# Retention and a gelu feed-forward on one core: spreading the retention steps over the first blocks, with steps 10-13 turned by DMA, the state cast on ScalarE and the last row block in halves

## The chip, the cores and the metric

The kernel runs on one core of a Trainium2 chip. TensorE (PE in the profile) multiplies, VectorE (DVE) and ScalarE (ACT) do the elementwise work, GpSimd (POOL) and SyncE (SP) issue transfers. Each engine takes its own list of instructions in order, and semaphores tie the lists together. The metric is the time of the whole kernel on the device, in microseconds (us); lower is better.

## The reference

```python
# q, k, v: (8 batches, 8 heads, 576 positions, 64)
scores = (q @ k.transpose(0, 1, 3, 2)) / sqrt(64)
gamma  = 1 - 2.0 ** (-5 - arange(8))                    # one decay per head
D      = where(i - j >= 0, gamma[h] ** (i - j), 0)      # causal decay
attn   = (scores * D) @ v
x = attn.transpose(0, 2, 1, 3).reshape(4608, 512)
h = x @ w_in                                            # (4608, 2048)
out = (h / (1 + exp(-1.702 * h))) @ w_out               # (4608, 512)
```

## The kernel before

**Retention in steps.** Each batch's 576 positions are five pieces of 128, 128, 128, 128 and 64 rows, so there are 40 *steps*; step n is piece n % 5 of batch n // 5. The decay is split into a factor per query row (`gq`), a factor per key row (`vfac`, multiplied into v by `scale_v`, line 314) and a causal mask. A running *state* (keys times values, summed over pieces in `zacc`) carries the earlier pieces. For a step the kernel needs:

- q and k *turned*, so that the 64 head values lie on partitions. Before step 14 (`PE_TURNS`) that is eight transposes on TensorE into the bank `psW` and an evacuation on ScalarE (`transposes`, line 338, and `evac_t`, line 344; together `turn`). From step 14 on SP issues two DMA transposes (`dma_turn`, line 545). The result is in one of four `qk` buffers.
- the scores on TensorE (line 375) and the mask on VectorE (line 397): together `intra`.
- `values_quarters` (lines 416 to 435): mask times v, the state's update and the earlier state's contribution, into `psV`, in two parts with the next step's `intra` between them.
- `finish`: `evac_o` (line 535) writes the step's rows into `xT` times `gq`; `evac_z` (lines 506 to 521) adds the new state to `zacc` and, after the first three pieces, casts `zacc` to the bf16 buffer `zq` that the next step reads. After a batch's last step `finish` also has POOL load a later batch.

`burst(n)` puts these together: step n-1's values, step n's scores and mask, the turn of step n+1 (or the DMA turn of step n+3), `finish(n-1)` and `scale_v(n+1)`.

**Feed-forward in blocks.** The 4608 rows are nine *blocks* of 512. A block's first product (`hidden`, line 593, 16 units of four matmuls of 512 columns) goes through the gelu on ScalarE (line 598) into `gT`. `hidden_half` (line 611) does the same in 16 units of eight matmuls of 256 columns, the first eight for the block's first half of rows. The second product (`project`, line 627, 16 units: four row blocks r, four quarters g) ends each row block with a copy out of PSUM on VectorE (line 635) and an output transfer on SP.

**Banks.** Hidden units take turns over `psH0`, `psH1` and, with three in rotation, `psU`, by a counter `hcount` that runs through the whole kernel. `project(0)` uses `psU`, `psH0`, `psH1` and `psU` again for its fourth row block; in later blocks row blocks alternate between `psU` and `psW`. The last block uses four banks.

**Order.** The order is written out by hand: each call records instructions on every engine's list, and `Rec` works out the semaphore waits from what is read, written and which bank is touched. Steps 0 to 3 come first, then block 0's first product, block 0's second product with steps 4 to 7, block 1's first product with bursts 8 to 13, and then regions:

```python
between = {0: 8, 2: 9, 5: 10, 8: 11, 11: 12, 14: 13}
for i in range(NF):
    hidden_half(1, i // 8, 2 * (i % 8))
    if i in between:
        burst(between[i])
```

`region(c)` (line 751) interleaves block c-1's second product with block c's first in 32 units, in the repeating pattern O H O H O O H H (O for `project`, H for `hidden`), and places its four or five bursts evenly. Region 2 holds bursts 14 to 18; regions run to 8, and the last block's second product ends the kernel.

Of the kernel before, what the change touches and what calls it, by code (L numbers as in the profile page):

```python
# [6 lines left out]
AF = mybir.ActivationFunctionType  # L7
# [15 lines left out]
NCH = (B * S) // 512  # L23
NF = FF // 128
NST = 3
NQK = 4
PE_TURNS = 14
QK_SCALE = 1.0 / math.sqrt(DH)


# [99 lines left out]
def bass_retnet_parallel__then__act_gelu_quick_kernel(  # L130
# [9 lines left out]
    R = Rec()  # L140
    es = ExitStack()
    with es:
        def sb(name, shape, dtype):
            return es.enter_context(nc.sbuf_tensor(name, shape, dtype))

        def ps(name, shape, dtype=FP32):
            return es.enter_context(nc.psum_tensor(name, shape, dtype))
# [12 lines left out]
        zacc = sb("zacc", [P, HP, DH], FP32)  # L160
        zq = [sb(f"zq{i}", [P, HP, DH], BF16) for i in range(2)]
# [9 lines left out]
        w_out_sb = sb("w_out_sb", [P, NF, DM], BF16)  # L171
        gT = [sb(f"gT{i}", [P, NF, 512], BF16) for i in range(2)]
        osb = [sb(f"osb{i}", [P, 512], FP32) for i in range(3)]

        psW = ps("psW", [P, 512])
        psT = psW.ap().bitcast(BF16).rearrange("p (a h n) -> p a h n", a=2, h=HP)
        psS = ps("psS", [P, 2, HP, 128])
        psV = ps("psV", [P, 2, 512])
# [135 lines left out]
        def scale_v(n, eng="DVE"):  # L314
            b, c = divmod(n, NC)
            sl = b % NST
            t = st_v[:, sl, c, :].rearrange("p (h d) -> p h d", d=DH)
            f = vfac[min(b, 1)][:, :, c : c + 1].to_broadcast([P, H, DH])
            R.op(eng, lambda e: e.tensor_tensor(t, t, f, ALU.mult),  # L319
                 r=[("vfac", min(b, 1))], w=[("v", sl, c)])  # L320
# [26 lines left out]
        def turn_first_keys():  # L347

            transposes(4, [(1, st_k, "k", 1, 0)])
            R.op("ACT", lambda e: e.activation(qk[4 % NQK][:, 1], psT[:, 1], AF.Copy),  # L350
                 w=[("qk", 4 % NQK, 1)], ps=["W"])
# [154 lines left out]
        def evac_z(n):  # L506
            c = n % NC
            if n >= NC:
                new = psV[:, :, 256:384]
                acc = zacc.ap().rearrange("p (u t) d -> p u (t d)", u=2)  # L510
                z = zq[c % 2].ap().rearrange("p (u t) d -> p u (t d)", u=2)
                if c == 0:
                    R.op("DVE", lambda e: e.tensor_copy(acc, new), w=["zacc"], ps=["O", "Z"])
                elif c < 3:
                    R.op("DVE", lambda e: e.tensor_tensor(acc, acc, new, ALU.add),
                         w=["zacc"], ps=["O", "Z"])
                if c < 3:
                    R.op("DVE", lambda e: e.tensor_copy(z, acc), r=["zacc"], w=[("zq", c % 2)])
                else:
                    R.op("DVE", lambda e: e.tensor_tensor(z, acc, new, ALU.add),  # L520
                         r=["zacc"], w=[("zq", c % 2)], ps=["O", "Z"])
                return
            for hh in range(2):
                rows = slice(64 * hh, 64 * hh + 64)
                R.op("ACT", lambda e, rows=rows: e.activation(
                    zs[c % 2][rows, :, rows], psZ[rows, :, 0:64], AF.Copy),
                    w=[("zs", c % 2, hh)], ps=["Z"])
# [17 lines left out]
        def dma_turn(n):  # L545
            for a, t, nm, sl, c in sides(n):
                rows = P if nm == "k" else ROWS[c]
                R.op("SP", lambda e, a=a, t=t, rows=rows, sl=sl, c=c: e.dma_start_transpose(
                    out=qk[n % NQK][:, a, :, 0:rows], in_=t[0:rows, sl, c, :]),
                    r=[(nm, sl, c)], w=[("qk", n % NQK, a)], dma=("turn", n % NQK, a))  # L550

        def turn(n):
            transposes(n)
            evac_t(n)
# [5 lines left out]
        def finish(n):  # L560
            evac_o(n)
            if n % NC < 4:
                evac_z(n)
            b = n // NC + NST
            if n % NC == 4 and b < B:
                load_entry(b)

        def burst(n):
            if n > NC:
                values_quarters(n - 1)  # L570
            else:
                intra(n)
                values(n - 1)
            if n + 1 < PE_TURNS:
                turn(n + 1)
            if PE_TURNS <= n + 3 < NSTEP:
                dma_turn(n + 3)
            finish(n - 1)
            if n + 1 < NSTEP:
                scale_v(n + 1)  # L580


        hcount = [0]
# [2 lines left out]
        def hidden(c, f, rotate=2):  # L586
            bank, key = hbanks[hcount[0] % rotate]
            hcount[0] += 1
            toks = {(t0 // S, (t0 % S) // 128) for t0 in range(512 * c, 512 * c + 512, 64)}

            def fn(e):
                for a in range(4):
                    i = e.matmul(bank.ap(), w_in_sb[:, a, 128 * f : 128 * f + 128],  # L593
                                 xT[:, a, 512 * c : 512 * c + 512],
                                 start=(a == 0), stop=(a == 3))
                return i
            R.op("PE", fn, r=[("w_in", f // 4)] + [("xT", *x) for x in sorted(toks)], ps=[key])
            R.op("ACT", lambda e: e.activation(gT[c % 2][:, f, :], bank.ap(),  # L598
                                               AF.Gelu_apprx_sigmoid),
                 w=[("gT", c % 2, f)], ps=[key])  # L600
# [20 lines left out]

        ocount = [0]

        def project(c, r, g, bank, key):
            def fn(e):
                for f in range(4 * g, 4 * g + 4):
                    i = e.matmul(bank, gT[c % 2][:, f, 128 * r : 128 * r + 128], w_out_sb[:, f, :],  # L627
                                 start=(f == 0), stop=(f == NF - 1))
                return i
            R.op("PE", fn, r=[("w_out", g)] + [("gT", c % 2, f) for f in range(4 * g, 4 * g + 4)],  # L630
                 ps=[key])
            if g == 3:
                m = ocount[0] % 3
                ocount[0] += 1
                R.op("DVE", lambda e: e.tensor_copy(osb[m].ap(), bank), w=[("osb", m)], ps=[key])  # L635
                row0 = 512 * c + 128 * r
                R.op("SP", lambda e: e.dma_start(out[row0 : row0 + 128, :], osb[m].ap()),
                     r=[("osb", m)], dma=("osb", m))


        constants_first()
# [66 lines left out]
        for b in (1, 2):  # L708
            load_entry(b)

        wide = [(psU.ap(), "U"), (psH[0].ap(), ("H", 0)), (psH[1].ap(), ("H", 1)),
                (psV[:, 0, :], "O")]
# [8 lines left out]
        def burst_4():  # L721
            intra(4)
            turn_first_keys()
            turn(5)
            scale_v(5)

        def burst_7():
            values_quarters(6)
            finish(6)
            turn(8)  # L730
            scale_v(8)

        regroup()
        between = {6: turn_4, 8: burst_4, 10: lambda: burst(5), 12: lambda: burst(6),
                   14: burst_7}
        units = [(r, g) for g in range(4) for r in range(3)] + [(3, g) for g in range(4)]
        for i, (r, g) in enumerate(units):
            project(0, r, g, *wide[r % 3])
            if i in between:
                between[i]()  # L740
        between = {0: 8, 2: 9, 5: 10, 8: 11, 11: 12, 14: 13}
        for i in range(NF):
            hidden_half(1, i // 8, 2 * (i % 8))
            if i in between:
                burst(between[i])

        def last_step(c):
            t = 512 * (c + 1) - 1
# [2 lines left out]
        def region(c):  # L751
            units = []
            for r in range(4):
                o = [("O", c - 1, r, g) for g in range(4)]
                h = [("H", c, f) for f in range(4 * r, 4 * r + 4)]
                units += [o[0], h[0], o[1], h[1], o[2], o[3], h[2], h[3]]
            if c + 1 < NCH:
                bursts = list(range(last_step(c) + 2, last_step(c + 1) + 2))
            else:
                bursts = []  # L760
            at = {}
            for i, n in enumerate(bursts):
                at[int((i + 0.5) * (len(units) - 2) / len(bursts))] = n
            for i, u in enumerate(units):
                if u[0] == "H":
                    hidden(u[1], u[2])
                else:
                    project(u[1], u[2], u[3], *(wide[0], (psW.ap(), "W"))[u[2] % 2])
                if i in at:
                    burst(at[i])  # L770

        for c in range(2, NCH):
            region(c)
        for r in range(4):
            for g in range(4):
                project(NCH - 1, r, g, *wide[r])


        R.number()
# [55 lines left out]
```

## Time and profile before

| what | value |
|---|---|
| median of 3 runs | 311.97 us (311.85 to 314.23) |
| the profiled execution | 311.36 us, span 309.6 us |
| PE / DVE / ACT / POOL busy | 294.7 / 144.4 / 111.7 / 155.5 us |
| granted TensorE clock | 0.999 of full speed |
| region 3 begins on PE at | 108.45 us |
| last output copy begins at | 306.37 us |

Busy time adds up instructions; a busy TensorE is not one at its peak, because matmuls overlap. A line of the groups gives the line of the kernel, engine, operation, what is written and read, shapes and count; then the busy time in us and the mean of one in ns; then the engine's idle time just before these instructions and who ended it. A line of the timeline gives start and length in us, and in brackets the idle time before it and its releaser.

### The profile page before, as it was taken

The numbers are of one execution on the slowest core, as the hardware profiler recorded it, in microseconds if no ns is written. First come the engines' busy times: TensorE is split into PE (matmuls) and PEld (weight loads), VectorE is DVE, ScalarE is ACT, GpSimd is POOL, SyncE is SP. The second block draws the span as 40 slices with busy tenths as digits, with TensorE's granted clock in tenths as the row PEclk, the third lists the DMA queues.
The fourth block names the chain that finished last, engine by engine and source line by source line (L and its number), as shares of the span: only waits on it lengthen the run. The fifth ranks groups of instructions, "written<-read, shape, count | busy, mean of one in ns | idle before, by whom it ended". The sixth has DMA issues, their size and how long they took to land.

```text
span 309.6 us, 7171 instructions
## 1 busy us (share of the span) xinstructions
PE 294.7 (95%) x3132; PEld 150.8 (49%) x3171; DVE 144.4 (47%) x241; ACT 111.7 (36%) x186; POOL 155.5 (50%) x208
## 2 busy tenths in 40 slices
PE   8789988899999999999999999999999999999995
PEld 3444454787444444444444444444444444444442
DVE  7761658857537643544346443435354441100011
ACT  8676233475232323333223333333333333333300
POOL 9999999999999999999660000000000000000000
PEclk9999999999999999999999999999999999999999
DMA  9999999999999999999993223223330000101011
GB/s 72 152 199 200 185 152 202 172 115 114 153 184 156 156 181 165 171 155 169 172 142 76 71 70 86 61 53 85 70 78 36 34 36 34 37 36 66 34 70 68
DMA packets 149280, 34.57 MB, mean 112 GB/s; under 512 B 140544, under 2 KB 144640, under 8 KB 149248
## 3 DMA queue, kind: packets, MB, share of 16 engines
q0 software_dynamic: 117856, 18.36, 89.2%
q1 hardware_dynamic: 31392, 15.74, 23.1%
q8 instruction: 25, 0.41, 0.6%
q14 instruction: 7, 0.06, 0.1%
HBM read 36.70 MB, written 9.44 MB: 149 GB/s over the span
## 4 chain that ended last, share of the span: by engine, by line
PE 88%; DVE 4%; POOL 2%; issue 2%; DMA 1%; ACT 1%; POOLq 0%
PE psH L593 34%; PE psU L627 18%; PE psW L627 15%; PE psH L627 4%; PE psV L416 4%; PE psH L611 2%; PE psS L375 2%; DVE sm L397 2%; DMA st_k<-in_k_dram 1%; PE psU L593 1%; PE psW L338 1%; POOL st_q L198 1%; PE psV L435 1%; PE psV L627 1%; PE psV L428 1%
## 5 line engine op out<-in xcount | busy, mean ns | idle before, releaser
L598 ACT ACTIVATE gT<-psH 128x512 bf16<-128x512 f32 x123 | 73.4, 597 | 151.5 <-PE psH L593 151.5
L593 PE MATMUL psH<-xT,w_in_sb 128*128 128x512 bf16 x481 | 118.9, 379 | 2.1 <-issue 1.3
L397 DVE TENSOR_TENSOR sm<-psS,mask 128x1024 bf16<-128x1024 f32 (+1 forms) x40 | 44.7, 1117 | 87.4 <-PE psS L375 83.6
L593 PEld LDWEIGHTS psH<-xT,w_in_sb 128*128 128x128 bf16 x492 | 47.2, 98 | 57.0 <-DVE xT L541 0.6
L211 POOL DMA_DIRECT2D st_k<-in_k_dram x70 | 66.8, 1186 | 4.4 <-PE psV L435 4.2
L211 POOL DMA_DIRECT2D st_v<-in_v_dram x70 | 66.6, 1189 | 0.0
L627 PE MATMUL psU<-w_out_sb,gT 128*128 128x512 bf16 x258 | 64.2, 379 | 1.7 <-issue 1.4
L627 PE MATMUL psW<-w_out_sb,gT 128*128 128x512 bf16 x214 | 53.1, 379 | 1.5 <-issue 1.4
L198 POOL DMA_DIRECT2D st_q<-in_q_dram x40 | 51.5, 1288 | 0.1
L627 PEld LDWEIGHTS psU<-w_out_sb,gT 128*128 128x128 bf16 x272 | 25.6, 98 | 29.7 <-ACT gT L598 0.3
L627 PEld LDWEIGHTS psW<-w_out_sb,gT 128*128 128x128 bf16 x224 | 21.1, 98 | 24.9
L319 DVE TENSOR_TENSOR st_v<-st_v,vfac 128x512 bf16<-128x512 bf16 x37 | 25.2, 681 | 1.0 <-DMA st_v<-in_v_dram 1.0
L635 DVE COPY osb<-psU 128x512 f32<-128x512 f32 x17 | 11.7, 689 | 28.6 <-PE psU L627 28.6
L535 DVE TENSOR_TENSOR xT<-psV,gq 128x512 bf16<-128x512 f32 (+1 forms) x35 | 22.0, 628 | 4.2 <-PE psV L435 4.2
L344 ACT ACTIVATE qk<-psW 128x1024 bf16<-128x1024 bf16 x14 | 14.3, 1023 | 20.7 <-PE psW L338 20.7
L416 PE MATMUL psV<-sm,st_v 64*64 64x64 bf16 (+1 forms) x504 | 17.5, 214 | 1.9 <-DVE st_v L319 1.7
L635 DVE COPY osb<-psW 128x512 f32<-128x512 f32 x14 | 9.6, 687 | 18.6 <-PE psW L627 18.6
L416 PEld LDWEIGHTS psV<-sm,st_v 64*64 64x64 bf16 x504 | 9.1, 105 | 16.7 <-issue 11.9
L627 PE MATMUL psH<-w_out_sb,gT 128*128 128x512 bf16 x62 | 14.4, 379 | 0.1
L428 PE MATMUL psV<-st_v,st_k 64*64 64x64 bf16 x448 | 13.0, 192 | 0.0
L435 PE MATMUL psV<-qk,zq 64*64 64x128 bf16 (+1 forms) x224 | 12.6, 215 | 0.1
L611 PE MATMUL psH<-xT,w_in_sb 128*128 128x256 bf16 x88 | 11.4, 273 | 0.2 <-DVE xT L535 0.2
(89 smaller groups left out, 198.7 us busy)
## 6 DMA issues: line engine op xcount, KB each, us to landing
out_dram<-osb SPq DMA_DIRECT2D x36, 256.0 KB, 2.4
st_q<-in_q_dram POOLq DMA_DIRECT2D x32, 128.0 KB, 6.4
st_k<-in_k_dram POOLq DMA_DIRECT2D x57, 64.0 KB, 6.3
st_v<-in_v_dram POOLq DMA_DIRECT2D x57, 64.0 KB, 6.1
w_in_sb<-in_moe_w_in_dram POOLq DMA_DIRECT2D x4, 512.0 KB, 8.1
w_out_sb<-in_moe_w_out_dram POOLq DMA_DIRECT2D x4, 512.0 KB, 13.9
st_k<-in_k_dram POOLq DMA_DIRECT2D x4, 128.0 KB, 4.4
st_v<-in_v_dram POOLq DMA_DIRECT2D x4, 128.0 KB, 4.6
```

The source lines that it names most:

```text
L198: R.op("POOL", lambda e, d=d, s=s: e.dma_start(d, s), w=[(nm, sl, c)], dma=(nm, sl, c))
L211: R.op("POOL", lambda e: [e.dma_start(d, s) for d, s in parts], w=[(nm, sl, c)], dma=(nm, sl, c), parts=2)
L319: R.op(eng, lambda e: e.tensor_tensor(t, t, f, ALU.mult), r=[("vfac", min(b, 1))], w=[("v", sl, c)])
L397: R.op("DVE", lambda e: e.tensor_tensor(o, i, m, ALU.mult), r=[("mask", 0), ("mask", 1)] if b else [("mask", 0)], w=[("sm", n % 3)], ps=["S"])
L416: i = e.matmul(psV[half(t), u, 128 * j + 64 * last : 128 * j + N], st_v[rows, sl, cc, 64 * h : 64 * h + 64], s[rows, j, 2 * t + u, 64 * la ...
L428: i = e.matmul(psV[half(j), u, 256 + 64 * t : 320 + 64 * t], st_k[rows, sl, cc, hs], st_v[rows, sl, cc, hs], start=False, stop=False, skip ...
L535: R.op("DVE", lambda e: e.tensor_tensor(xT[:, :, t0 : t0 + N].rearrange("p (u j) n -> p u j n", u=2), psV[:, :, 0:256].rearrange("p u (j n ...
L593: i = e.matmul(bank.ap(), w_in_sb[:, a, 128 * f : 128 * f + 128], xT[:, a, 512 * c : 512 * c + 512], start=(a == 0), stop=(a == 3))
L598: R.op("ACT", lambda e: e.activation(gT[c % 2][:, f, :], bank.ap(), AF.Gelu_apprx_sigmoid), w=[("gT", c % 2, f)], ps=[key])
L611: m = e.matmul(bank[:, 256 * i : 256 * i + 256], w_in_sb[:, a, 128 * (f + i) : 128 * (f + i) + 128], xT[:, a, a0 : a0 + 256], start=(a == ...
L627: i = e.matmul(bank, gT[c % 2][:, f, 128 * r : 128 * r + 128], w_out_sb[:, f, :], start=(f == 0), stop=(f == NF - 1))
L635: R.op("DVE", lambda e: e.tensor_copy(osb[m].ap(), bank), w=[("osb", m)], ps=[key])
```

## The change

- `PE_TURNS` goes from 14 to 10: steps 10 to 13 are turned by DMA. An extra `dma_turn(10)` is placed in `burst_7`.
- The state's cast `zacc` to `zq` moves from VectorE to ScalarE.
- In `burst`, `scale_v(n + 1)` comes before `finish(n - 1)`. In `burst_7` the old order stays.
- Block 0's four output copies go to ScalarE, and the turn of step 5 comes one unit later.
- Block 1's second product now stands between block 1's first and block 2's first, instead of being interleaved with the latter. Bursts 8 to 18 are spread over the three (three, three and five of them). Block 2's first product rotates over three banks. Regions begin with 3.
- The last row block is computed as two halves of 256 columns in two banks, each with its own copy and output transfer.

```diff
-PE_TURNS = 14
+PE_TURNS = 10
...
                 if c < 3:
-                    R.op("DVE", lambda e: e.tensor_copy(z, acc), r=["zacc"], w=[("zq", c % 2)])
+                    R.op("ACT", lambda e: e.activation(z, acc, AF.Copy),
+                         r=["zacc"], w=[("zq", c % 2)])
...
-            finish(n - 1)
             if n + 1 < NSTEP:
                 scale_v(n + 1)
+            finish(n - 1)
...
+                if eng == "ACT":
+                    R.op("ACT", lambda e: e.activation(osb[m].ap(), bank, AF.Copy),
+                         w=[("osb", m)], ps=[key])
...
+        def project_halves(c, r, banks):
+            row0 = 512 * c + 128 * r
+            for i, (bank, key) in enumerate(banks):
+                cols = slice(256 * i, 256 * i + 256)
+                def fn(e, bank=bank, cols=cols):
+                    for f in range(NF):
+                        m = e.matmul(bank[:, 0:256], gT[c % 2][:, f, 128 * r : 128 * r + 128],
+                                     w_out_sb[:, f, cols], start=(f == 0), stop=(f == NF - 1))
+                    return m
...
+                R.op("DVE", lambda e, bank=bank, m=m: e.tensor_copy(
+                    osb[m][:, 0:256], bank[:, 0:256]), w=[("osb", m)], ps=[key])
...
         def burst_4():
             intra(4)
             turn_first_keys()
+
+        def turn_5():
             turn(5)
             scale_v(5)
...
             turn(8)
+            dma_turn(10)
             scale_v(8)
...
-        between = {6: turn_4, 8: burst_4, 10: lambda: burst(5), 12: lambda: burst(6),
+        between = {6: turn_4, 8: burst_4, 9: turn_5, 10: lambda: burst(5), 12: lambda: burst(6),
                    14: burst_7}
...
-            project(0, r, g, *wide[r % 3])
+            project(0, r, g, *wide[r % 3], eng="ACT")
...
-        between = {0: 8, 2: 9, 5: 10, 8: 11, 11: 12, 14: 13}
+        between = {1: 8, 5: 9, 11: 10}
         for i in range(NF):
             hidden_half(1, i // 8, 2 * (i % 8))
             if i in between:
                 burst(between[i])
+        pair = [wide[0], (psW.ap(), "W")]
+        between = {0: 11, 5: 12, 10: 13}
+        for i in range(16):
+            project(1, i // 4, i % 4, *pair[i // 4 % 2])
+            if i in between:
+                burst(between[i])
+        between = {0: 14, 3: 15, 7: 16, 10: 17, 13: 18}
+        for f in range(NF):
+            hidden(2, f, 3)
+            if f in between:
+                burst(between[f])
...
-        for c in range(2, NCH):
+        for c in range(3, NCH):
             region(c)
-        for r in range(4):
+        for r in range(3):
             for g in range(4):
                 project(NCH - 1, r, g, *wide[r])
+        project_halves(NCH - 1, 3, [(psV[:, 0, :], "O"), (psW.ap(), "W")])
```

## The prediction

> **What bounds the kernel now.** First the page: how busy each engine is, and the chain of waits that ended last. Then the groups by shape.
>
> ```profile
> PE 294.7 (95%) x3132; PEld 150.8 (49%) x3171; DVE 144.4 (47%) x241; ACT 111.7 (36%) x186; POOL 155.5 (50%) x208
> ...
> PE 88%; DVE 4%; POOL 2%; issue 2%; DMA 1%; ACT 1%; POOLq 0%
> ...
> L598 ACT ACTIVATE gT<-psH 128x512 bf16<-128x512 f32 x123 | 73.4, 597 | 151.5 <-PE psH L593 151.5
> ```
>
> TensorE (PE) is the chain for 88% of the span, and ScalarE (ACT) idles before its gelus. So a change pays only where it shortens PE's instruction stream or a PE wait, and costs only where it makes a wait. The PE timeline of the stage that is rearranged shows both:
>
> ```profile
> 54.16 1.04 PE L611 MATMUL psH<-xT,w_in_sb 128*128 128x256 bf16 x8 [0.24 <-DVE xT L535]
> 55.48 0.31 PE L416 MATMUL psV<-sm,st_v 64*64 64x128 bf16 x8 [0.27 <-DVE st_v L319]
> ...
> 56.29 0.40 PE L338 MATMUL psW<-ident,st_q 128*128 128x128 bf16 x4
> 56.52 0.39 PE L338 MATMUL psW<-ident,st_k 128*128 128x128 bf16 x4
> 56.74 1.04 PE L611 MATMUL psU<-xT,w_in_sb 128*128 128x256 bf16 x8
> 57.62 1.04 PE L611 MATMUL psH<-xT,w_in_sb 128*128 128x256 bf16 x8
> 59.34 0.31 PE L416 MATMUL psV<-sm,st_v 64*64 64x128 bf16 x8 [0.68 <-DVE st_v L319]
> ```
>
> A unit of eight 256-column matmuls takes 0.87 us (57.62 minus 56.74 is 0.88), a unit of four 512-column ones 0.86, a step's two transposes 0.45 (56.29 to 56.74). Call the start of a burst B: burst 8 is B = 55.48. A burst without transposes takes 0.82 us, 0.70 for the first step of a batch and 0.52 for the last, plus a gap of 0.09 before it (all read off the PE timeline). Between bursts the VectorE (DVE) chain must run:
>
> ```profile
> 56.13 1.23 DVE L397 TENSOR_TENSOR sm<-psS,mask 128x1024 bf16<-128x1024 f32 x1
> 57.28 0.68 DVE L535 TENSOR_TENSOR xT<-psV,gq 128x512 bf16<-128x512 f32 x1
> 57.87 0.41 DVE L515 TENSOR_TENSOR zacc<-zacc,psV 128x256 f32<-128x256 f32 x1
> 58.32 0.37 DVE L518 CAST zq<-zacc 128x256 bf16<-128x256 f32 x1
> 58.61 0.67 DVE L319 TENSOR_TENSOR st_v<-st_v,vfac 128x512 bf16<-128x512 bf16 x1
> ```
>
> The mask starts at B+0.65, and the last item ends at 59.28, B+3.80; PE goes on 0.06 later. Two or three units after a burst do not cover that; four do.
>
> **The gains.** (a) Steps 10 to 13 leave PE: 4 x 0.45 = **-1.8**. Their eight DMA transposes go to SP, whose existing ones hold SP 1.2 us each and land in a median of 4.8 us, at most 7.3. Steps 10 to 13 are asked for three bursts ahead, at least 11 us here by the spacing below, so nothing waits. Step 10's, issued in `burst_7`, stand on SP ahead of one output row and wait for the reads of step 6's `qk`, done in that burst; that row is needed by nobody soon. Software loads lead their use by 10 us or more there (the batch with step 15 is issued from 63 us, used near 90), so eight more transfers beside them cost 0. Without that cover each late turn would cost its lateness once. POOL refills a batch's buffers when its last step is finished: step 9 is now finished in burst 10 near 68.6 instead of 63.3, and POOL starts that refill (batch 4) only at 81.7, so POOL loses 0.
> (b) Wider spacing removes the waits before bursts 8, 9 and 12: the gaps on PE are 0.45, 0.85 and 0.22, of which 0.09 each is ordinary: 0.36+0.76+0.13 = **-1.25**.
> (c) In `project(0)` four DVE copies of 0.69 go to ScalarE. Burst 5 is now behind `evac_t(5)` on ScalarE (one unit, not two, lies between), and the mask of step 5 no longer waits for two copies (its start, 45.58, was 0.71 after the scores). Walked through, burst 5 starts near 44.45 instead of 44.87, and burst 7 at 51.25 instead of 51.63: **-0.38**. Moving `turn(5)` one unit later fills the 0.69 wait on `qk L350`, but `evac_t(5)` behind the row copy gives about 0.4 of it back; that is inside the 0.38.
> (d) The tail:
>
> ```profile
> 302.72 3.62 PE L627 MATMUL psV<-w_out_sb,gT 128*128 128x512 bf16 x15
> 302.92 0.69 DVE L635 COPY osb<-psH 128x512 f32<-128x512 f32 x1 [2.76 <-PE psH L627]
> 306.37 0.69 DVE L635 COPY osb<-psV 128x512 f32<-128x512 f32 x1 [2.76 <-PE psV L627]
> ```
>
> The last copy shrinks from 0.69 to the 0.415 of a 128x256 copy out of PSUM (`L513`). The last transfer, 2.4 us for 256 KB, is halved: between 0 and 0.3 less, since loads of 64 and 32 KB land in the same 6.1 to 6.3 us; I take 0.1. The matmuls go from 16 x 0.216 to 32 x 0.109, +0.03. Sum **-0.35**.
> Gains together: -3.8.
>
> **The costs.** The cast of the state goes to ScalarE, where it is recorded in `finish`, ahead of all later gelus. ScalarE runs its list in order, so it now stands still until the DVE chain reaches `zacc`. And `scale_v` moves ahead, so `zacc` ends 0.60 later: B+0.65+1.14+0.60+0.59+0.41 = B+3.40 (0.05 less after a batch's first step). The cast has no row on ScalarE; nearest are these two of 256 elements and of 512:
>
> ```profile
> L525 ACT ACTIVATE zs<-psV 64x256 bf16<-64x256 f32 x8 | 3.0, 376 | 0.9 <-PE psV L473 0.8
> L598 ACT ACTIVATE gT<-psH 128x512 bf16<-128x512 f32 x123 | 73.4, 597 | 151.5 <-PE psH L593 151.5
> ```
>
> I take 0.38, at most 0.60. The cast then runs from B+3.45 to B+3.83, the first gelu behind it from 3.80 to 4.40, and PE can reuse that bank at B+4.45. The DVE's cast has a mean of 0.381, so nothing is won in length. The Trainium skill ("ScalarE: Activation LUTs", Rules for kernel authors) advises VectorE for adds and simple arithmetic, being up to three times faster per element; the equal durations here do not bear that out for this cast. By that rule the cast would be three times its 0.38, 1.1 us, and the eight waits below would each grow by 0.75, making the sum 6 us higher.
> (e) Second half unit of block 1. It writes `psU`, which holds `project(0)`'s last row block. Its copy is now on ScalarE behind `cast(6)` and `evac_t(8)`. `zacc` ends at B+2.80 in burst 7 (there `finish` comes first); cast starts 2.85, evacuation 3.20, copy 4.12, PE goes on at 4.77. It would have been ready at 2.52+0.87 = 3.39. **+1.38**.
> (f) After burst 8 four half units on three banks: the fourth needs the first's gelu, at 4.45, against 1.26+3x0.87 = 3.87: **+0.58**.
> (g) Bursts 17 and 18 stand three units after their predecessors and need the cast, which lets PE go at 3.88 (3.83 after burst 16, a first step); PE would be ready at 0.70+3x0.86+0.09 = 3.38 and 0.82+2.59+0.09 = 3.50: **+0.83**. Bursts 11 to 13 have four or five units: 0.
> (h) `hidden(2)` now rotates over three banks and its last unit, hidden counter 47, lands in `psU`. The next PE unit, `project(2)` row 0, also writes `psU`. Behind burst 18's cast stand the gelus of the last two units: starts 3.80 and 4.37, end 4.97, PE at 5.02, against 0.82+2x0.86 = 2.55: **+2.47**. It is not made up later, since PE never idles afterwards.
> (i) Blocks 3 to 7 use two banks. The third hidden unit after a burst needs the first's gelu, B+4.45. By `region`'s positions, bursts with a cast at place 18 or 26 (21, 22, 31) leave H O O H in between, 0.82+4x0.86 = 4.27, or 4.15 after a first step: 0.25+0.18+0.25. Burst 26 at place 21 leaves H H O: 4.40-3.29 = 1.11. The others are covered by O units. **+1.8**.
> Costs: 7.06. Each contains one cast; at 0.60 instead of 0.38 the eight places cost 1.8 more. A cast at 0 would take 3 off.
>
> **Sum.** -3.8+7.1 = +3.3. The profiled execution takes 311.36 us (span 309.6, 1.8 around it), so 314.7; the median of the three runs is 311.97, 0.6 above, so the forecast is **315.3**. About 1% (3.1 us) is what a measurement of this kernel can tell from no change, and the forecast sits just beyond it.
>
> **The rivals.**
> *Slow cast*: at 0.60 the sum is +5.1, 317.1. For it: the DVE cast itself is 0.83 in one instance (129.27). Against: both ScalarE rows scale smoothly with elements.
> *Spreading wins* (other side): the wider spacing hides the whole chain, ScalarE's stand costs nothing, and only the gains are left: 308.2. It needs `zacc` earlier. Each of eight waits would have to be 0.41 shorter for zero change, 0.8 for over 1% faster. For it: ScalarE is idle for 64%. Against: the same chain, added up in the old order, gives burst 8's start to within 0.06, and (h) stays at 0.7 even with no cast at all.
> *Part of it*: ScalarE reaches the row copy or the gelus in time, and (e) or (h) falls out: +1.9 or +0.8, about 313.3. For it: 64% idle again. Against: the bank names are fixed by counters.
> *Late turns*: the transposes of steps 10 to 13 land after their burst. One that is late by 2 us gives 317.3. Against: 11 us ahead, 7.3 worst landing.
> *The clock falls*: one wait of 2.5 us is three times the longest PE idle after the first 2 us now (0.77), with granted clock 1.00. The opening shows a slow start: 14 idle matmuls in 5.18 us instead of 14x0.216 = 3.0, so a relapse costs 2.2: 317.5. The Trainium skill ("TensorE: Matmul & The Clock Gate", Part 1) puts the drop after a window of about 3.4 us without work; no run here shows one yet.
>
> **Chances.** Forecast 0.64, slow cast 0.12, spreading wins 0.08, part 0.08, late turns 0.03, clock 0.05. The forecast's own spread is about 1 us, so it splits 0.36 over and 0.28 under 1%. Slower: 0.36+0.12+0.03+0.05 = 0.56; same: 0.28+0.08 = 0.36; faster 0.08. Range 311.4 to 317.6: up to the clock rival, down to (e) and (h) both gone (-0.6), and leaving the faster rival out.
>
> **What would show it.** Right: a PE wait of some 2.5 us on a gelu before `project(2)`, near 108 us; one of 1.4 before the second half unit of block 1; `zq` casts on ACT near 0.4 us; ACT waits for `zacc`; transposes on PE down by four steps; `psV` waits gone at bursts 8, 9, 12; region 4 with a wait near 1.1. Wrong: no PE wait on ACT above 0.5 us, casts much longer, or PE waiting for `qk` by DMA.

## The result, and the profile after

The changed kernel takes 316.88 us (median; 316.72 to 317.35) against 311.95 of the kernel before (four runs each): 4.9 us more, a ratio of 1.0143 with a 95% interval of 1.0095 to 1.0190. The profiled execution has a span of 314.9 us (before 309.6). The forecast was 315.3, slower: right in direction and inside its range, with the time 1.6 above it.

The page of the kernel after, in the lines that answer to those of before (share of the span by engine, the chain by engine, the cast's group):

```profile
PE 301.5 (96%) x3155; PEld 150.9 (48%) x3155; DVE 134.8 (43%) x217; ACT 116.0 (37%) x207; POOL 155.7 (49%) x208
...
PE 84%; DVE 6%; POOL 3%; ACT 2%; DMA 2%; issue 1%; POOLq 0%
...
L518 ACT ACTIVATE zq<-zacc 128x256 bf16<-128x256 f32 x21 | 8.7, 416 | 62.3 <-DVE zacc L515 40.8
```

ScalarE is still idle for 63% of the span, but 2% of the chain is now its own, and it stood 62 us in front of its 21 casts. Who waits for that is in the list of waits (engine, line, what it waited for; us in total, times, longest):

```profile
PE psU L628 <- ACT gT L599: 2.2, 1, 2.2
PE psV L416 <- ACT zq L518: 1.8, 3, 0.9
...
PE psU L612 <- ACT osb L637: 1.1, 1, 1.1
...
PE psH L594 <- ACT gT L599: 1.0, 1, 1.0
...
PE psH L612 <- ACT gT L618: 0.4, 1, 0.4
```

None of these five stood in the list of before, where PE waited for ScalarE in three rows, all ahead of burst 7:

```profile
PE psS L364 <- ACT qk L344: 1.4, 3, 0.6
...
PE psW L338 <- ACT qk L350: 0.7, 1, 0.7
...
PE psH L485 <- ACT zs L525: 0.2, 1, 0.2
```

(The longest of the three waits on `zq`, 0.91, stands before burst 7, where before had 0.77 on another releaser.) In the PE timeline the others are where the working put them: the second half unit of block 1, the fourth after burst 8, bursts 17 and 18, the start of region 3, and burst 26's third hidden unit:

```profile
56.40 1.05 PE L612 MATMUL psU<-xT,w_in_sb 128*128 128x256 bf16 x8 [1.13 <-ACT osb L637]
...
61.78 1.05 PE L612 MATMUL psH<-xT,w_in_sb 128*128 128x256 bf16 x8 [0.35 <-ACT gT L618]
...
101.87 0.31 PE L416 MATMUL psV<-sm,st_v 64*64 64x128 bf16 x8 [0.49 <-ACT zq L518]
...
105.87 0.31 PE L416 MATMUL psV<-sm,st_v 64*64 64x128 bf16 x8 [0.43 <-ACT zq L518]
...
111.00 1.04 PE L628 MATMUL psU<-w_out_sb,gT 128*128 128x512 bf16 x4 [2.24 <-ACT gT L599]
111.87 1.69 PE L594 MATMUL psH<-xT,w_in_sb 128*128 128x512 bf16 x4
113.35 1.91 PE L628 MATMUL psU<-w_out_sb,gT 128*128 128x512 bf16 x4
115.06 1.25 PE L594 MATMUL psH<-xT,w_in_sb 128*128 128x512 bf16 x4
...
169.88 1.04 PE L594 MATMUL psH<-xT,w_in_sb 128*128 128x512 bf16 x4 [0.99 <-ACT gT L599]
```

The bracket counts idle time from the modelled end of the matmul before. How much later a unit starts than it could have is a little more: 107.73 plus 0.86 is 108.59, so region 3 starts 2.41 us late. The sums below use this lateness.

The three lines after 111.00 show something else: units of four 512-column matmuls start 1.48 and 1.71 us apart, where 0.86 is usual. The table by windows says why (stretch; busy time and count of PE, PEld, DVE, ACT, POOL; then the granted clock, the DMA share and GB/s):

```profile
111.00:112.00 1.00, 1.00 (x5) 0.50 (x6) 0.00 (x0) 0.00 (x0) 1.00 (x3) 1.00 2.30 157
112.00:113.00 1.00, 1.00 (x5) 0.35 (x3) 0.00 (x0) 0.00 (x0) 1.00 (x3) 0.55 1.78 156
113.00:114.00 1.00, 1.00 (x4) 0.37 (x3) 0.00 (x0) 0.41 (x1) 1.00 (x4) 0.50 1.69 150
114.00:115.00 1.00, 1.00 (x3) 0.29 (x2) 0.00 (x0) 0.19 (x1) 1.00 (x3) 0.50 1.72 153
115.00:116.00 1.00, 1.00 (x5) 0.36 (x3) 0.00 (x0) 0.00 (x0) 1.00 (x3) 0.75 2.36 150
```

After the long wait the clock is at half speed for 3.4 us (0.45 + 0.50 + 0.50 + 0.25 us were lost, 1.7 in all). All four executions of this kernel show a mean clock of 0.995, but only this one has a trace that shows where it fell; the profiled execution of before has 0.999.

The two profiles, cut at four points of the PE and VectorE timelines, add up (in before, the unit behind burst 19 lacks the record of its first matmul, and its start, 112.81, is set one matmul ahead of the first record):

| stretch | before | after | difference |
|---|---|---|---|
| start to block 1's first half unit | 54.16 | 54.23 | +0.07 |
| to region 3's first unit | 54.29 | 56.77 | +2.48 |
| to the unit behind burst 19 | 4.36 | 6.05 | +1.69 |
| to the start of the last output copy | 193.56 | 195.30 | +1.74 |
| to the end of the span | 3.20 | 2.58 | -0.62 |
| span | 309.57 | 314.93 | +5.36 |

### The profile page after: what moved, and what is told of

It reads as the page before. It is cut to its first block, busy times and chain, and to the rows that moved or that the text cites. A ratio compares the mean times of both kernels' runs of the same rounds, so it can differ in the third digit from the quotient of the medians.

```text
span 314.9 us, 7190 instructions
## 1 busy us (share of the span) xinstructions
PE 301.5 (96%) x3155; PEld 150.9 (48%) x3155; DVE 134.8 (43%) x217; ACT 116.0 (37%) x207; POOL 155.7 (49%) x208
## 4 chain that ended last, share of the span: by engine, by line
PE 84%; DVE 6%; POOL 3%; ACT 2%; DMA 2%; issue 1%; POOLq 0%
PE psH L594 31%; PE psU L628 18%; PE psW L628 15%; PE psH L628 4%; PE psV L416 4%; DVE sm L397 3%; DMA w_in_sb<-in_moe_w_in_dram 2%; PE psH L612 2%; PE psU L594 2%; PE psS L375 2%; DVE xT L536 1%; POOL st_q L198 1%; PE psU L612 1%; DVE st_v L319 1%; POOL st_k L198 1%; PE psV L435 1%
## 5 line engine op out<-in xcount | busy, mean ns | idle before, releaser
L594 PE MATMUL psH<-xT,w_in_sb 128*128 128x512 bf16 x468 | 116.6, 382 | 1.7 <-ACT gT L599 1.0
L599 ACT ACTIVATE gT<-psH 128x512 bf16<-128x512 f32 x117 | 69.5, 595 | 95.9 <-PE psH L594 94.7
L211 POOL DMA_DIRECT2D st_k<-in_k_dram x70 | 67.5, 1202 | 8.6 <-PE psV L435 8.6
L594 PEld LDWEIGHTS psH<-xT,w_in_sb 128*128 128x128 bf16 x468 | 44.5, 98 | 56.0 <-ACT gT L599 3.0
L628 PE MATMUL psU<-w_out_sb,gT 128*128 128x512 bf16 x272 | 67.5, 383 | 2.2 <-ACT gT L599 2.2
L628 PE MATMUL psW<-w_out_sb,gT 128*128 128x512 bf16 x224 | 54.8, 379 | 0.0
L198 POOL DMA_DIRECT2D st_q<-in_q_dram x40 | 52.3, 1308 | 0.1
L518 ACT ACTIVATE zq<-zacc 128x256 bf16<-128x256 f32 x21 | 8.7, 416 | 62.3 <-DVE zacc L515 40.8
L640 DVE COPY osb<-psU 128x512 f32<-128x512 f32 x15 | 10.3, 688 | 25.9 <-PE psU L628 25.6
L344 ACT ACTIVATE qk<-psW 128x1024 bf16<-128x1024 bf16 x10 | 10.2, 1022 | 12.1 <-PE psW L338 12.1
L435 PE MATMUL psV<-qk,zq 64*64 64x128 bf16 (+1 forms) x224 | 12.9, 215 | 0.1
```

Source lines behind the costliest of these rows:

```text
L198: R.op("POOL", lambda e, d=d, s=s: e.dma_start(d, s), w=[(nm, sl, c)], dma=(nm, sl, c))
L211: R.op("POOL", lambda e: [e.dma_start(d, s) for d, s in parts], w=[(nm, sl, c)], dma=(nm, sl, c), parts=2)
L435: i = e.matmul(psV[half(t), u, 128 * j : 128 * j + N], zq[(c - 1) % 2][half(j), 2 * u + t, :], qk[n % NQK][half(j), 0, 2 * u + t, 0:N], st ...
```

## The experiments

The theory: ScalarE, in order, stands at the cast until `zacc` is there, and gelus and copies behind it hold banks that TensorE needs; the longest such wait also costs the clock. The rivals: the transposes by DMA, or the new spacing, cost the time. Because the stretch before burst 7 varies by itself (last section), profiles are also compared from the start of burst 7 to the end of the span: 257.9 us before, 263.2 after.

**The cast back on VectorE.** Edit of the changed kernel:

```diff
-                    R.op("ACT", lambda e: e.activation(z, acc, AF.Copy),
-                         r=["zacc"], w=[("zq", c % 2)])
+                    R.op("DVE", lambda e: e.tensor_copy(z, acc), r=["zacc"], w=[("zq", c % 2)])
```

> The changed kernel with the state's cast back on VectorE, nothing else. Theory (ScalarE stands at the cast and holds the gelus, the row copy and the banks behind it): the waits of 1.30 us on psU in block 1, 0.52 on the fourth half unit and 1.69 in regions 3 to 5 vanish, the 2.41 us wait before region 3 shrinks to about 0.75 (the last unit's gelu alone), the clock stays up there (1.70 us), the waits before bursts 17 and 18 (1.0 together) stay, since the chain is as long on VectorE: 316.9 - 6.9 = 310.0. Rival (the transposes by DMA and the later loads, or the spread bursts, are what costs): 316 or more, with waits on transfers.

Measured: 309.78 us, ratio 0.9933 (0.9908 to 0.9958) to the kernel before. With all the other edits in place, this one costs 7.1 us (256.2 from burst 7 on, against 263.2), 1.7 of them through the clock, and the rest of the change is faster than before by 2.1. What is left of PE's waits for gelus and casts, from its list:

```profile
PE psV L416 <- DVE zq L518: 1.5, 3, 0.7
...
PE psU L627 <- ACT gT L598: 0.7, 1, 0.7
...
PE psH L593 <- ACT gT L598: 0.2, 1, 0.2
```

The 0.7 is region 3's start, as expected without a cast; the 1.5 holds 0.70 before burst 7 and the 0.28 and 0.49 before bursts 17 and 18 (0.77 together, where 1.0 was expected). The waits on `psU` in block 1 and in the regions are gone, and the clock is 1.000. The rival falls: the transposes by DMA are still in this kernel.

**The bank of block 2's last unit.** The changed kernel with one line ahead of block 2's first product:

```diff
+        hcount[0] += 2
```

> The changed kernel with the bank counter moved on by 2 before block 2's first product, so that its last two units land in psH0 and psH1 and not in psU; the cast stays on ScalarE. Theory: region 3's first unit starts without waiting, its second (a hidden unit in psH0) waits about 1.0 us for the gelu held by the cast, in place of 2.41; with the shorter wait the granted clock stays at 1.00 near 110 us: 316.9 - 1.4 - 1.7 = 313.8. Rival (the clock falls for another reason, such as the long stretch of small matmuls): 315.5.

Measured: 313.66 us, ratio 1.0051 (1.0032 to 1.0069), clock 1.000. Region 3's first unit starts with no wait, the second waits as worked out:

```profile
108.38 1.03 PE L628 MATMUL psU<-w_out_sb,gT 128*128 128x512 bf16 x4
110.39 1.02 PE L594 MATMUL psH<-xT,w_in_sb 128*128 128x512 bf16 x4 [0.98 <-ACT gT L599]
```

A name of a bank was worth 3.2 us, about half of it through the clock.

**An idle TensorE and its clock.** Two kernels put matmuls on zeros into the 2.24 us of idle time before region 3, nine in the first and two in the second (n is 9 or 2):

```diff
+        def idle_fill(e):
+            for _ in range(n):
+                m = e.matmul(psW.ap(), idle[:, 0:128], idle.ap(), start=True, stop=True)
+            return m
+        R.op("PE", idle_fill, r=["idle"], ps=["W"])
         for c in range(3, NCH):
             region(c)
```

> The changed kernel with nine matmuls on zeros into psW (9 x 0.216 = 1.94 us) put between block 2's first product and region 3, inside the 2.41 us wait on psU. They compute nothing that is used. Theory (an idle TensorE is what loses the clock): region 3 still starts near 111.0 on the wait for the gelu, but the clock stays at 1.00 and the 1.70 us come back: 315.2. Rival (the clock falls for another reason): 316.9. Second rival (the fill delays region 3): up to 318.8.

> The changed kernel with two matmuls on zeros (0.43 us, computing nothing that is used) in front of region 3, so that TensorE idles about 1.8 us there in place of 2.24. Theory (it is the length of the idle stretch that loses the clock, and 1.64 held it in the old-order run): the clock stays at 1.00 after region 3's start and the time is 315.2. Rival (1.8 is already too long): the clock halves again for 3 us and the time is 316.9.

Measured: 315.50 us with nine (ratio 1.0118, 1.0085 to 1.0151) and 315.61 with two (1.0114, 1.0081 to 1.0148), 1.4 and 1.3 below the changed kernel. From burst 7 on both profiles take 261.7, 1.5 below it. The wait for the gelu is still there, now split into fill and rest, and the clock there holds. With two:

```profile
108.77 0.59 PE L815 MATMUL psW<-idle 128*128 128x512 bf16 x2
111.18 1.04 PE L628 MATMUL psU<-w_out_sb,gT 128*128 128x512 bf16 x4 [1.81 <-ACT gT L599]
112.05 1.03 PE L594 MATMUL psH<-xT,w_in_sb 128*128 128x512 bf16 x4
```

So the clock's fall follows TensorE's idle time and is a term of its own: with 0.43 us of useless work in front of the wait it did not come. The profiled execution with nine has a clock of 0.995 all the same: it lost it near 20 us, at the start of the first product. Four of the six executions with nine and seven of the ten with two have a clock of 1.00, against none of the four without a fill.

**Only the transposes by DMA.** The kernel before with `PE_TURNS = 10` and `dma_turn(10)` in `burst_7`, nothing else.

> The kernel before with steps 10 to 13 turned by DMA, nothing else. Theory: TensorE loses 4 x 0.45 us and all transposes land in time; before bursts 9 and 10 to 12 the VectorE chain leaves a part of it as a wait, because bursts 9 to 12 stand only two or three units apart (burst 9's own turn is no cover for its start, but those of bursts 11 and 12 are: their successors were just in time): -0.9 to -1.8, so 310.2 to 311.1. Rival (DMA transposes in the loaded phase come late or slow the loads): 312 or more.

Measured: 315.55 us, ratio 1.0097 (1.0066 to 1.0127). In the profile, 2.6 us of the loss lie behind the start of burst 7 and 0.8 ahead of it, where nothing was edited. My expectation was wrong; the rival is right that in the old order the transposes come late. From the list of PE's waits, and then the timelines of SP (the issue) and PE (the use) for step 11's keys:

```profile
PE psV L416 <- DVE st_v L319: 2.5, 5, 0.7
PE psV L435 <- issue: 1.7, 1, 1.7
...
PE psS L375 <- DMA qk<-st_k: 1.3, 2, 1.0
```

```profile
59.16 1.41 SPq L548 DMA_TRANSPOSE qk<-st_k x1
...
68.29 0.43 PE L375 MATMUL psS<-qk 64*64 64x128 bf16 x16 [1.02 <-DMA qk<-st_k]
```

Three bursts ahead is only some 11 us there, SP issues the keys' transposes 2.9 us after burst 8 began, and between 50 and 80 us they land 6.8 to 9.4 us after the issue. Two waits on the VectorE chain are new as well, 0.63 and 0.22 before bursts 12 and 13, which the transposes on TensorE had covered. The 1.7 us on `L435` is a pause inside one group of matmuls for which the profile shows no releaser; its cause stays open, and without it this profile would be 0.9 above before from burst 7 on. So the late transposes and these waits explain why the gain of 1.8 is gone, and not the whole of the loss. In the new order bursts 8 and 11 lie some 16 us apart, and no PE wait on a transpose by DMA is left.

**Only the cast and the order.** The kernel before with the cast on ScalarE and `scale_v` ahead of `finish`.

> The kernel before with two edits: the state's cast on ScalarE and scale_v ahead of finish in burst; all else as before. Theory: the third hidden unit after a burst waits for a gelu that stands behind the cast: 1.69 us in regions 3 to 5 as in the changed kernel, about 1.15 in region 2 (burst 17 stands at place 21 there), and some 0.3 in block 1's half units: 311.9 + 3.1 = 315.0. Rival (the cast hurts only together with the new spacing and banks of blocks 1 and 2): 311.9 to 312.5.

Measured: 315.74 us, ratio 1.0106 (1.0069 to 1.0142); from burst 7 on 261.5, 3.6 above before (3.1 expected). Cast and order cost without the new spacing too, so the rival falls. The surplus shows in two waits I had put at 0 and smaller: 0.42 on `xT` at the start of block 2's first product, which `evac_o` behind `scale_v` writes later, and 0.92 in place of 0.68 before burst 9.

**The order alone undone.** The changed kernel with `finish` ahead of `scale_v` again, cast on ScalarE.

> The changed kernel with finish ahead of scale_v in burst again, the cast still on ScalarE. Theory: zacc ends 0.60 earlier, so ScalarE stands shorter. The fourth half unit after burst 8 and regions 3 and 5 no longer wait, burst 26 waits 0.5, bursts 17 and 18 about 0.1, region 3's start 1.84 in place of 2.41, block 1's psU still 1.3: 316.9 - 3.2 = 313.7, and 312.0 if the clock holds through a wait of 1.84. Rival (only the cast's engine matters, not the order): 316 or more.

Measured: 313.32 us, but spread from 311.25 to 315.62, ratio 1.0019 (0.9985 to 1.0053). By the median this is not decided between 312.0 and 313.7; the six executions with a clock of 1.00 lie between 311.25 and 312.96. The trace is clearer, 259.0 from burst 7 on, 4.2 below the changed kernel where 4.9 was expected with the clock held, and it holds two pauses of 0.47 and 0.51 for which it shows no releaser. Region 3 starts after a wait of 1.6 us, and the clock there holds:

```profile
PE psU L628 <- ACT gT L599: 1.6, 1, 1.6
...
PE psU L612 <- ACT osb L637: 0.8, 1, 0.8
...
PE psH L594 <- ACT gT L599: 0.6, 2, 0.4
```

So cast and order work on each other: `scale_v` ahead makes ScalarE's cast start 0.60 later (burst 17: 3.44 us after its start against 2.84). With the cast on VectorE the same change of order is worth only 0.7 us (the third version below).

**Better versions.** The first takes the cast back to VectorE, moves the counter on by 2 and gives the full VectorE chain four units (`{0: 14, 3: 15, 6: 16, 10: 17, 14: 18}`). The second is the same with steps 10 to 13 on TensorE, and block 1's second product in `psU` and `psH0`. The third is the first with `finish` ahead of `scale_v`.

> The changed kernel with the cast on VectorE, the bank counter moved on by 2 before block 2's first product, and bursts 16 and 18 moved to units 6 and 14 there, so that the full VectorE chain has four units to run under. Theory: against the 309.8 of the version with the cast on VectorE alone, the wait of 0.69 before region 3 and those of 0.28 and 0.49 before bursts 17 and 18 vanish: 308.3. Rival (the waits move on to another bank or to transfers): 309.8.

> As the run beside it (cast on VectorE, counter moved on, bursts at units 6 and 14), but with steps 10 to 13 turned on TensorE as before the change, and block 1's second product in psU and psH0, since psW then takes the transposes. Theory: with bursts four units apart the DMA transposes cost nothing, so taking them back adds 4 x 0.45 us: 1.8 above its neighbour, 310.1. Rival (the transposes by DMA slow the loads, as they did in the old order, and cost what they save): equal to its neighbour within 0.5, or below it.

> The best version so far (cast on VectorE, counter moved on, bursts at units 6 and 14) with finish ahead of scale_v again. Theory: with the cast on VectorE the order inside the chain changes nothing for the next burst, but xT is written 0.60 earlier, so the wait of 0.43 that region 3's first hidden unit had on xT goes: 0.4 less from burst 7 to the end of the span (255.0 to 254.6). Rival (scale_v late costs more than xT early gains): equal or above 255.0.

| version | median us | ratio to before (interval) | burst 7 to end |
|---|---|---|---|
| first | 309.23 | 0.9884 (0.9837 to 0.9931) | 255.0 |
| second, transposes on TensorE | 310.82 | 0.9955 (0.9922 to 0.9987) | 256.7 |
| third, old order | 308.24 | 0.9858 (0.9810 to 0.9906) | 254.3 |

In the spread order the DMA transposes earn 1.7 us from burst 7 on, close to their 1.8, by one profile each (the medians differ by 1.6). The first version's medians stand 0.9 above the expectation, with single runs from 307.92 to 310.36; its trace shows the wait on `xT` of 0.43 that the third removes (0.7 gained, 0.4 expected). The third beats both kernels, by 3.7 us against before.

## Why the prediction was right, and where it was not

- **What bounds the kernel** held: every difference above is one of PE's stream, of a PE wait or of PE's clock.
- **(a) and (b)**: between the first half unit and region 3 the waits of the change are 1.30 + 0.52 + 0.55 + 0.51 + 2.41 = 5.29 us, and the stretch grew by 2.48, so the gains there are 2.81 against 3.05. In (a) the step "eight more transfers beside them cost 0" failed in part. The loads became much slower to land (before, after, and with the transposes alone in the old order):

```profile
st_q<-in_q_dram POOLq DMA_DIRECT2D x32, 128.0 KB, 6.4
```

```profile
st_q<-in_q_dram POOLq DMA_DIRECT2D x32, 128.0 KB, 10.2
```

```profile
st_q<-in_q_dram POOLq DMA_DIRECT2D x32, 128.0 KB, 13.1
```

The lead of 10 us or more took this up in the changed kernel, so PE waited for none of them behind block 0's first product. The cover named in the prediction was the right one; with less spacing the lead of the transposes was not enough.
- **(c)**: -0.27 against -0.38 (burst 7 at 51.69 with a front 0.33 later, against 51.63).
- **(d)**: -0.62 against -0.35. The copy took 0.42, as priced. The halved transfer landed in 1.7 us, and the last full one of before had taken 2.0, not the median of 2.4 that the working used: 0.3, the top of what I had allowed, in place of 0.1. These two make 0.57 of it.
- **(e) to (h)**: 1.30, 0.52, 1.06 and 2.41 against 1.38, 0.58, 0.83 and 2.47. The cast was 0.416, not 0.38. For the same cast VectorE took 0.295 in the median, and 0.381 in the mean because a few took up to 0.83. The Trainium skill ("ScalarE: Activation LUTs", Rules for kernel authors) gives VectorE up to about three times the speed per element for bf16 operations with one source; this cast reads fp32, so neither the 1.1 us that the prediction worked out from the rule nor the measured ratio of 1.4 is a test of it. What made the cast dear was its place in ScalarE's list.
- **(i)**: the four waits of regions 3 to 5 are 0.20, 0.14, 1.15 and 0.20, together 1.69; the stretch grew by 1.74 against 1.8. The waits of the sum are nine in all and not the eight of the rivals' prices: one each in (e), (f) and (h), two in (g), four in (i). The slow cast should thus have stood at 317.3.
- **The step that failed** is the clock, which the sum left at full speed: as a rival it had a chance of 0.05. It was priced at 2.2 and took 1.70; its condition, one long wait, was a term of my own sum (h). The longest idle stretch that had held the clock, 0.77, could say nothing about one of 2.5. The time, 316.88, lies nearer to this rival's 317.5 than to the forecast, and the range holds it with its upper end set at that rival. The rest of the sum, +3.3, is what the trace gives without the clock and without the front: 5.36-1.69-0.33 = 3.3.

## What to carry to other kernels

An instruction put on a mostly idle in-order engine costs what stands behind it while it waits: go through the bank or buffer that each later instruction frees, and through every place where a counter decides the bank. A short operation belongs on the engine that has just produced its input, or behind the work that others wait for. Whether work can move to the DMA queues depends on how far ahead it can be asked for once the queues are loaded, not on its landing time in the quiet stage.

## What the runs showed of the hardware

- At region 3 the clock fell after PE had idled 2.24 us and held after 1.81 and 1.64. The Trainium skill ("TensorE: Matmul & The Clock Gate", Part 1) gives an idle window of about 3.4 us; in the traced execution a shorter idle time was enough.
- The length of the idle time alone does not decide. Before block 0's first product the clock held after 1.65 us in the run with the transposes alone, and fell after 1.17 in the run with nine matmuls on zeros. The kept traces record every change of the clock: after the opening, in all twelve, the changes lie whole multiples of 3.41 us apart, and each of the five falls inside a kernel lasts one such stretch. An estimate from the matmul records (0.216 us for 512 columns, times the part of the 128 by 128 array in use) puts the array's share in the stretch ahead of each fall at 0.25 to 0.35. The lowest of all others, up to the last 10 us of a kernel, has 0.40. So, as far as these traces go, a wait costs the clock when it and small matmuls together leave well over half of one such stretch unused. At region 3 the 2.24 us all lay in one stretch, 108.68 to 112.09 us. The stretches begin at another place in each execution, so this need not hold in every one.
- The front of the kernel differs from run to run: PE's idle time before block 0's first product is 0.77 us in the profile of before and 0.64 to 2.38 in the others, with the same code up to there. (Where only seven of the first eight matmuls have a record, 0.22 of it is the missing one.) In the four profiles in which the clock fell there, after 1.17, 1.75, 1.81 and 2.38, burst 7 starts at 53.4 to 54.4 us, in the others at 51.5 to 52.6. A first product that starts late can thus cost 1 to 3 us, which is as much as the edits under study.
- Eight more transposes by DMA, in a stage in which the page shows the DMA engines nine tenths busy, raised the median landing of the software loads: from 6.4 us to 13.1 in the old order, and from 8.7 to 15.1 in the spread order with the cast on VectorE. The spread order without them thus has slower loads too. In the changed kernel the 128 KB loads landed in 12.9 us between 100 and 130 us (6.7 before), and still in 10.1 between 130 and 180, where the loads end (5.4 before).
